# One core, attention followed by two expert layers: loads laid out as single stretches, the first expert of the second layer picked from an incomplete sum, and routing steps placed later

## The chip, the cores and the metric

The kernel runs on one core of one Trainium2 chip. The metric is the device time of one execution in microseconds (us), and lower is better. The median of three runs of the kernel before is 150.59 us (150.51 to 150.84).

## The reference

The computation has three parts, one after the other, on 1536 tokens of 512 numbers (float32).

1. A decaying linear attention over blocks of 64 positions gives `x`.
2. A soft mixture of 8 experts with 4 slots each: `slot_input = softmax_over_tokens(x @ phi).T @ x`, then per expert `relu(slot_input[e] @ w1[e]) @ w2[e]`, then `x = softmax_over_slots(x @ phi) @ slot_out`. The weights `moe_w1` and `moe_w2` are 32 MB.
3. A hard mixture of 8 experts: each token goes to the expert with the largest gate, at most `capacity` = 384 tokens per expert, others stay zero:

```
expert_idx = argmax(x @ w_gate)
h = relu(disp @ w1); y = h @ w2
out[i] = gate_w[i] * y[expert_idx[i], pos[i]]   # kept tokens; other rows are 0
```

## The kernel before, in words

**Attention** (lines 182 to 273). Twelve units (6 stretches of 128 positions, 2 batches), written out by hand in one order for all engines (`manual_schedule`, line 335). For unit n the TensorE (PE) order is: scores, transposes of the next unit's k, transposes of the last unit's result, the product with the running state, the state's own update (`kv`, line 239), the product with v. VectorE (DVE) makes the decay tables `T` (line 168) from `lamf`, which lies in the small load `pgs`; each half of a unit's scores is multiplied with `T` (line 217), and `kd` (line 198) also needs `T`, so that in the first unit the first `kv` waits for `pgs`, both halves of `T` and `kd`.

**Loads.** All loads go through SyncE's (SP's) one queue, in order. A buffer of 1 MB (a "granule", `[128, 2, 1024]`) holds two units' worth of k, q or v, or a quarter of an expert's two matrices. Lines 94 to 103 load the first pair in pieces: k, q, `pgs` and v of batch 0 (256 KB each, 512 columns of each row of 2048), then k, q, v of batch 1, then the second column half (512 KB each). Lines 110 to 131 load the weights, 1 MB each; the last expert's `w2` is cut by columns into two pieces of 512 KB and four of 256 KB (line 122), which in memory are strips of the rows of one granule. The `Z`, `F` and `slt` steps (384 to 421) and the 16 `layer1`/`layer2` blocks (433 to 463) stream the 32 MB through PE.

**The last expert's layer 2** is done in three column parts: `layer2(7, 0)` makes columns 0 to 255 (bank `S[0]`), `layer2(7, 1)` columns 256 to 383 (`S[1]`, which holds all of columns 256 to 511 of the experts before), `layer2(7, 2)` columns 384 to 511 (`S[2]`). `sum_groups` (588) turns the scaled sums `Sp` into `SR`: the slots' outputs (three copies) and, in the last column, token 0's own output. `gate_slots` (592) multiplies the last column with `w_gate` into `l0` (token 0's eight gates) and the slots with `w_gate` into `gp`.

**Choice of the first expert** (620 to 627). The arg max of `l0` goes through a register on SP (`value_load`), and `load_expert` issues this expert's 4 MB in ten pieces (571 to 575): `w1` and `w2` in turn, four of 256 KB, then six of 512 KB. The write of zeros to the rows past `capacity` (`rest`, 565, 2304 KB) is issued on the same queue before them. If the choice were not the expert of all tokens, the loop at line 920 would run a pass for each other expert that has tokens.

**Routing on VectorE**: `gp` is copied to `G`, six matmuls `lps` (633) give all tokens' gates, then `rank_experts` (649), `first_gates` (657, with one Exp on ScalarE) and `split_gate` (667) follow ahead of `first_expert`. PE runs matmuls on zeros ("fillers", `keep_warm`, line 79) in the meantime.

**First expert** (714 to 837). Per quarter j: `project` (PE `pq`), ScalarE's rounded copy and VectorE's remainder `pr` (745), `add_parts` (PE `ph`, 750, needs `pr`), `pp`, `hidden` (PE `hq`, ScalarE `ht`, VectorE `ht` low part 774), the splitting of `w2` (ScalarE 754, VectorE 757), and the `output` matmuls (783). PE works these off in the written order, so `ph` of a quarter stands in front of the outputs that follow it. After quarter j one routing step is called (816): `count_tokens`, `rank_active`, `list_active`.

Fillers ahead of the first expert are counted in `WR`: `WR[3]` is 24.

Of the kernel before, what the change touches and what calls it, by code (L numbers as in the profile page):

```python
# [21 lines left out]
P = 128  # L22
# [10 lines left out]
NU = SEQ // P  # L33
NR = NU // 2
W0 = (20, 3, 5)
WR = (3, 2, 4, 24, 20)
WARM = (4, 2, 2, 3)
both = (0, 1)
BIG = 16384.0
SC = 32768.0  # L40
# [10 lines left out]
def tile_kernel(ctx: ExitStack, tc: tile.TileContext, q, k, v, pg, w1, w2,  # L51
# [34 lines left out]
    wgs = pgs[:, NK * NS:NK * (NS + NE)].rearrange("p (k s) -> p k s", k=NK)  # L86

    stage = []  # L90
    for u in range(0, NU, 2):
        pair = {nm: granule(f"{nm}st{u}") for nm in "kqv"}
        stage += [{nm: pair[nm][:, c].rearrange("p (b n) -> p b n", b=B) for nm in "kqv"} for c in range(2)]

        if u == 0:
            parts = [(0, slice(512 * b, 512 * b + 512)) for b in range(B)] + [(1, slice(0, 1024))]
        else:
            parts = [(slice(0, 2), slice(0, 1024))]
        for c, cols in parts:
            for nm, src in (("k", k), ("q", q), ("v", v)):  # L100
                nc.sync.dma_start(out=pair[nm][:, c, cols], in_=src[u // 2][:, c, cols])
                if nm == "q" and u == 0 and c == 0 and cols.start == 0:
                    nc.sync.dma_start(out=pgs, in_=pg)

    wtiles = {}
# [6 lines left out]
    def load_weights(n):  # L112
        for _ in range(n):
            if wnext[0] == len(wlist):
                return
            j0 = wnext[0]
            which, e, j = wlist[j0]
            wnext[0] += 1
            g = granule(f"w{which}_{e}_{j}", pool=pools[j0 % len(pools)])
            src = (w1 if which == 1 else w2)[e, j]  # L120

            n = (1 if (which, e) != (2, NE - 1) else (2, 4)[j])
            w = 2048 // n
            gf, sf = g.rearrange("p c n -> p (c n)"), src.rearrange("p c n -> p (c n)")
            for c in range(n):
                nc.sync.dma_start(out=gf[:, w * c:w * c + w], in_=sf[:, w * c:w * c + w])
            for c in range(2):
                t = g[:, c]
                if which == 2 and e < NE - 1:
                    t = t.rearrange("p (c n) -> p c n", c=2)  # L130
                wtiles[(which, e, 2 * j + c)] = t
# [318 lines left out]
    def layer2(e, j=None, fcs=range(NF)):  # L450
        for fc in fcs:
            g, a = fc // 2, fc % 2
            cg = fc % 4
            for z in range(2) if j is None else (j,):
                if j is None:
                    wt = wtiles[(2, e, g)][:, a, 256 * z:256 * z + 256]
                elif j == 0:
                    wt = wtiles[(2, e, fc // 4)][:, 256 * cg:256 * cg + 256]
                else:
                    wt = wtiles[(2, e, j + 1)][:, P * fc:P * fc + P]  # L460
                dst = S[z][32 * cg:32 * cg + 32, 0:P if j else 256]
                nc.tensor.matmul(dst, hTs[e][:, a, NS * g:NS * g + NS], wt,  # L462
                                 start=fc < 4 and (e == 0 or j == 2), stop=e == NE - 1 and fc >= 4)

    nst = cap // P
    layer1(0)
# [93 lines left out]
            for t in range(4):  # L560
                nc.vector.tensor_copy(stc[NS * t:NS * t + NS, 3 * NS:], cT[0:NS, 0, 0:1])


    rest = out[cap:, :].rearrange("(p r) d -> p r d", p=P)
    nc.sync.dma_start(out=rest, in_=bcast(zrow, 1, (NTOK - cap) // P))

    def load_expert(ev):
        m1, m2 = [granule("m1") for _ in range(2)], [granule("m2") for _ in range(2)]
        t1, t2 = [[g[:, c] for g in m for c in range(2)] for m in (m1, m2)]

        parts = [(t, 0, 512 * h, 512) for h in both for t in (t1, t2)]
        parts += [(t, j, 0, 1024) for j in range(1, 4) for t in (t1, t2)]
        for t, j, c, w in parts:
            src = mw1 if t is t1 else mw2
            nc.sync.dma_start(out=t[j][:, c:c + w], in_=src[ds(ev, 1), j, :, c:c + w].rearrange("e p n -> p (e n)"))  # L575
# [14 lines left out]
    def gate_slots(dst, lhs, kcs):  # L590
        for kc in kcs:
            nc.tensor.matmul(dst, lhs(kc), wgs[:, kc, :], start=kc == 0, stop=kc == NK - 1)

    e = NE - 1
    layer2(e, 0)
    nc.scalar.activation(Sp[:, 0:2].rearrange("p k n -> p (k n)"), S[0], AF.Copy, scale=rsum)
    layer2(e, 1)
    nc.vector.tensor_scalar(out=Sp[:, 2:4].rearrange("p k n -> p (k n)"), in0=S[1], scalar1=rsum,
                            scalar2=None, op0=ALU.mult)
    layer2(e, 2, range(4))  # L600
# [4 lines left out]
    nc.vector.scalar_tensor_tensor(out=Sp[:, 3], in0=S[2], scalar=rsum, in1=Sp[:, 3],  # L605
                                   op0=ALU.mult, op1=ALU.add)
    nc.scalar.copy(SR[:, 0:3], srp[0])

    keep_warm(WR[0], "qk", 2)
    sum_groups(3)  # L610
    nc.vector.tensor_copy(SR[:, 3:4], srp[1])
    y0 = lambda kc: SR[:, kc, 3 * NS:]
    slot = lambda kc: SR[:, kc, 0:NS]
    gate_slots(l0, y0, range(3))
    keep_warm(WR[1], "qk", 2)
    gate_slots(gp, slot, range(2))
    gate_slots(l0, y0, (3,))
    gate_slots(gp, slot, (2, 3))
    keep_warm(WR[2], "sc1")
    m0 = bpool.tile([1, NE], F32, name="m0")  # L620
    nc.vector.max(out=m0, in_=l0)
    e0i = bpool.tile([1, NE], U32, name="e0i")
    nc.vector.max_index(out=e0i, in_max=m0, in_values=l0)
# [19 lines left out]
    mx = bpool.tile([P, NT], F32, name="mx")  # L643
    vr = bpool.tile([P, NT, NE], F32, name="vr")
    vm = bpool.tile([P, NT], F32, name="vm")
    nc.vector.tensor_reduce(out=mx, in_=lgs, axis=AX.X, op=ALU.max)

    def rank_experts():
        nc.vector.tensor_tensor(out=vr, in0=lgs, in1=bcast(mx, 2, NE), op=ALU.is_equal)
        nc.vector.tensor_tensor(out=vr, in0=vr, in1=bcast(rank8, 1, NT), op=ALU.mult)  # L650
        nc.vector.tensor_reduce(out=vm, in_=vr, axis=AX.X, op=ALU.max)
# [62 lines left out]
    def first_expert(t1, t2):  # L714
# [81 lines left out]
        hidden(1)  # L796
        split_w2(1)
        hidden_low()
        for z in (1, 2):
            for s in range(nst):  # L800
                output(0, s, (z,))
        for j in range(3):
            project(j + 1)
            steps = [(2 * j, s) for s in range(nst) if j] + [(2 * j + 1, s) for s in range(nst)]
            for n, (fc, s) in enumerate(steps):
                output(fc, s)
                left = len(steps) - 1 - n
                if left == (3 if j else 2):
                    add_parts(j + 1)
                    split_w2(2 * j + 2)  # L810
                if left == (1 if j else 0):
                    for f in (2 * j + 2, 2 * j + 3):
                        hidden(f)
                        hidden_low()
                    split_w2(2 * j + 3)
            (count_tokens, rank_active, list_active)[j]()
        nv = nc.values_load(nact[0:1, 0:1], min_val=0, max_val=NE)
        for s in range(nst):
            output(NF - 2, s)
# [16 lines left out]
        keep_warm(WR[4], "lg")  # L836
        return nv

    rank_experts()
    first_gates()  # L840
    split_gate()
    nv = first_expert(*ew)
    ordered.close()

# [82 lines left out]
def arrays(inputs):  # L927
# [3 lines left out]
    named = [("q", heads["q"].reshape(B, NK, 2, NU, P, D).transpose(3, 2, 5, 0, 1, 4))]  # L931
    named += [(n, heads[n].transpose(2, 3, 0, 1, 4)) for n in "kv"]

    pairs = lambda a: np.reshape(a, a.shape[:-3] + (a.shape[-3] // 2, 2, P, 1024)).swapaxes(-3, -2)
    named = [(n, pairs(a.reshape(NU, P, B * DM))) for n, a in named]

    pg = [np.reshape(inputs[n], (NK, P, -1)).transpose(1, 0, 2).reshape(P, -1)
          for n in ("moe_phi", "moe2_w_gate")]
# [6 lines left out]
    w2 = np.concatenate([w2[:NE - 1], np.stack([a.reshape(P, 1024) for a in last])[None]])
    named += [("moe_w2", pairs(w2))]
    m1 = np.reshape(inputs["moe2_w1"], (NE, NK, P, 4, 2, P)).transpose(0, 3, 2, 4, 1, 5)
    m2 = np.reshape(inputs["moe2_w2"], (NE, 4, 2, P, DM)).transpose(0, 1, 3, 2, 4)
    named += [("moe2_w1", m1.reshape(NE, 4, P, 1024)), ("moe2_w2", m2.reshape(NE, 4, P, 1024))]
# [19 lines left out]
```

## Time and profile before

| what | value |
|---|---|
| median of 3 runs | 150.59 us (150.51 to 150.84) |
| the profiled execution's own time | 151.13 us |
| its span (first to last instruction) | 148.9 us |
| PE busy | 137.3 us (92%) |
| VectorE busy | 80.1 us (54%) |
| ScalarE busy | 43.1 us (29%) |
| mean granted PE clock | 0.985 of 2.4 GHz |
| moved by DMA | 50.70 MB, mean 341 GB/s |

The span starts with the first instruction and ends with the last; some 2.2 us of the execution's time lie around it. Engines: PE is the matmuls, PEld the weight loads of PE, which run ahead of them and show best when PE really waited; DVE is VectorE, ACT ScalarE, SPq the queue of SyncE that issues transfers. An arrow in brackets names what ended an engine's wait and how long the wait was. A transfer's rate is read from the table by stretches, where "DMA share" is the mean busy share of 16 DMA engines.

### The profile page before, as it was taken

How to read it: one execution, taken by the hardware profiler on the slowest of the kernel's cores; microseconds unless marked ns; L12 is line 12 of the kernel's file. 1: busy time of each engine (PE TensorE's matmuls, PEld its weight loads, DVE VectorE, ACT ScalarE, POOL GpSimd, SP SyncE). 2: the span in 40 equal slices, each digit the busy share in tenths (PEclk: the TensorE clock that was granted, in tenths of full speed). 3: DMA queues.
4: the chain of work that ended last, by engine and by line, in shares of the span. 5: the costliest groups of instructions: out<-in, count | busy, mean ns of one | idle time of the engine just before them, and what ended most of it. 6: DMA issues, size and time to landing. Idle time of an engine off the chain costs nothing.

```text
span 148.9 us, 4091 instructions
## 1 busy us (share of the span) xinstructions
PE 137.3 (92%) x1688; PEld 103.0 (69%) x1688; DVE 80.1 (54%) x193; ACT 43.1 (29%) x101; POOL 18.7 (13%) x39
## 2 busy tenths in 40 slices
PE   7829999999999999998899999999989898999990
PEld 5619888888688886976464665555647785778880
DVE  2496778966977896733437312111223645866810
ACT  3111424414233343234213001111112253463340
POOL 5004313440431200010003400000000000000000
PEclk9995999999999999999999999999999999999998
DMA  3899999999999999999999999999998889500041
GB/s 115 236 375 430 425 420 425 416 420 412 423 418 420 423 414 423 418 420 416 407 401 431 414 423 416 423 416 390 358 405 332 243 262 418 209 4 0 2 163 55
DMA packets 10692, 50.70 MB, mean 341 GB/s; under 512 B 1072, under 2 KB 1456, under 8 KB 6064
## 3 DMA queue, kind: packets, MB, share of 16 engines
q1 hardware_dynamic: 10528, 50.29, 85.2%
q8 instruction: 14, 0.23, 0.6%
q10 hardware_dynamic: 144, 0.13, 0.3%
q14 instruction: 6, 0.05, 0.1%
HBM read 47.27 MB, written 3.15 MB: 339 GB/s over the span
## 4 chain that ended last, share of the span: by engine, by line
PE 59%; DMA 26%; DVE 8%; SPq 2%; issue 2%; ACT 1%; DVEq 0%
DMA w<-in_moe_w_dram 19%; PE yp L783 9%; PE sp L209 8%; PE op L256 7%; PE op L228 7%; DMA m<-in_moe_w_dram 4%; PE kv L239 4%; PE hp L437 4%; PE kps L187 4%; PE xp L270 3%; PE wp L79 3%; DMA pgs<-in_pg_dram 3%; PE slp L320 2%; DVE T L168 2%; SPq L575 1%
## 5 line engine op out<-in xcount | busy, mean ns | idle before, releaser
L783 PE MATMUL yp<-wt,ht 128*128 128x512 f32 (+1 forms) x96 | 18.9, 342 | 0.0
L217 DVE TENSOR_TENSOR AT<-sp,T 128x512 f32<-128x512 f32 x24 | 15.5, 685 | 3.6 <-PE sp L209 3.1
L783 PEld LDWEIGHTS yp<-wt,ht 128*128 128x128 f32 x96 | 15.0, 189 | 3.3 <-DVE ht L774 0.5
L248 POOL TENSOR_TENSOR dec<-st,R 64x256 f32<-64x256 f32 x16 | 12.6, 785 | 34.2 <-DVE st L245 20.6
L462 PE MATMUL S<-w,hT 128*32 128x256 f32 (+1 forms) x272 | 16.4, 372 | 0.4 <-DMA w<-in_moe_w_dram 0.4
L437 PE MATMUL hp<-w,Z 128*32 128x256 f32 x256 | 15.5, 381 | 0.0
L209 PEld LDWEIGHTS sp<-qst,kT 64*128 64x128 f32 x192 | 12.3, 196 | 4.1 <-issue 1.8
L209 PE MATMUL sp<-qst,kT 64*128 64x128 f32 x192 | 14.6, 293 | 0.3 <-ACT kT L189 0.3
L256 PE MATMUL op<-AT,vst 128*64 128x128 f32 x192 | 13.7, 287 | 0.5 <-ACT xT L265 0.5
L79 PE MATMUL wp<-wsrc 128*128 128x256 bf16 x87 | 13.0, 300 | 1.1 <-DVE wsrc L74 1.1
L265 ACT COPY xT<-op 128x512 f32<-128x512 f32 (+1 forms) x13 | 7.2, 553 | 21.9 <-PE op L256 21.9
L462 PEld LDWEIGHTS S<-w,hT 128*32 128x32 f32 x272 | 8.7, 109 | 6.0 <-DMA w<-in_moe_w_dram 1.8
L189 ACT COPY kT<-kps 128x512 f32<-128x512 f32 x12 | 7.0, 586 | 18.6 <-PE kps L187 18.6
L256 PEld LDWEIGHTS op<-AT,vst 128*64 128x64 f32 x192 | 11.0, 145 | 1.0 <-ACT xT L265 0.7
L437 PEld LDWEIGHTS hp<-w,Z 128*32 128x32 f32 x256 | 8.3, 110 | 4.6 <-issue 0.2
L448 DVE COPY hT<-tp 128x256 f32<-128x256 f32 x8 | 3.3, 415 | 14.7 <-PE tp L446 14.7
L79 PEld LDWEIGHTS <-wsrc 128*128 128x128 bf16 x87 | 8.8, 108 | 3.2 <-DVE wsrc L74 1.1
L228 PE MATMUL op<-qd,st 128*128 128x128 f32 x80 | 10.9, 280 | 0.0
L245 DVE TENSOR_TENSOR st<-dec,kv 64x256 f32<-64x256 f32 x16 | 6.7, 419 | 7.1 <-PE kv L239 6.9
L228 PEld LDWEIGHTS op<-qd,st 128*128 128x128 f32 x80 | 9.7, 191 | 0.8 <-issue 0.8
L202 DVE TENSOR_TENSOR qd<-qst,R 128x512 f32<-128x512 f32 x10 | 9.8, 982 | 0.7 <-PE op L228 0.6
L187 PE MATMUL kps<-ident,kst 128*128 128x128 f32 x48 | 7.8, 285 | 1.7 <-DMA kst<-in_k_dram 1.7
(173 smaller groups left out, 160.5 us busy)
## 6 DMA issues: line engine op xcount, KB each, us to landing
w<-in_moe_w_dram SPq DMA_DIRECT2D x30, 1024.0 KB, 18.3
m<-in_moe_w_dram SPq DMA_DIRECT2D x6, 512.0 KB, 8.2
out_dram<-zrow SPq DMA_DIRECT2D x1, 2304.0 KB, 13.4
kst<-in_k_dram SPq DMA_DIRECT2D x2, 1024.0 KB, 12.4
qst<-in_q_dram SPq DMA_DIRECT2D x2, 1024.0 KB, 14.0
vst<-in_v_dram SPq DMA_DIRECT2D x2, 1024.0 KB, 15.0
w<-in_moe_w_dram SPq DMA_DIRECT2D x2, 512.0 KB, 18.1
w<-in_moe_w_dram SPq DMA_DIRECT2D x4, 256.0 KB, 13.0
```

The costliest lines, as they stand in the source:

```text
L79: nc.tensor.matmul(wp[:, 0:256], wsrc[:, 0:P], wsrc, start=True, stop=True)
L187: nc.tensor.transpose(ps[:, a, :], w["k"][:, P * a:P * a + P], ident)
L202: nc.vector.tensor_tensor(out=w["qd"], in0=w["q"], in1=R, op=ALU.mult)
L209: nc.tensor.matmul(sp[h2][:, a, :], w["kT"][hrows[h2], a, :], w["q"][hrows[h2], a, :], start=True, stop=True)
L217: nc.vector.tensor_tensor(out=t, in0=sp[h2], in1=tab, op=ALU.mult)
L228: nc.tensor.matmul(w["op"][:, a, :], st[b][:, a, :], w["qd"][:, a, :], start=a == 0, stop=False, skip_group_check=True)
L248: nc.gpsimd.tensor_tensor(out=dec[b][r], in0=st[b][r, :, r], in1=bcast(R[r, :, P - 1], 2, D), op=ALU.mult)
L256: nc.tensor.matmul(w["op"][hrows[h2], a, :], w["v"][:, D * (2 * a + h2):D * (2 * a + h2 + 1)], w["AT"][h2][:, a, :], start=u == 0 and a == ...
L265: nc.scalar.copy(xts[n][:, pairs], work[n]["op"][:, pairs])
L437: nc.tensor.matmul(hp[32 * g:32 * g + 32, :], Zf[:, kc, NS * e:NS * e + NS], wtiles[(1, e, kc)][:, 256 * g:256 * g + 256], start=kc == 0, ...
L462: nc.tensor.matmul(dst, hTs[e][:, a, NS * g:NS * g + NS], wt, start=fc < 4 and (e == 0 or j == 2), stop=e == NE - 1 and fc >= 4)
L783: nc.tensor.matmul(dst, ht[:, a, P * s:P * s + P], rhs, start=(fc, z) == (0, 0), stop=(fc, z) == (NF - 1, 2))
```

## The change

Every DRAM array is laid out on the host so that each load reads one unbroken stretch; the tiles in on-chip memory stay as they are. The first k, q and v are now loaded by 512 KB (both batches at once) and `pgs` stands behind k and q of that size. The expert's ten pieces become eight: `w1` and `w2` in turn, of 256, 256, 512 and 1024 KB.

The first expert is now chosen from `yg`, token 0's output without the last expert's share in columns 256 to 511: `guess_first` uses `Sp[:, 0:2]` and `Sg`, a scaled copy of `S[1]` before `layer2(7, 1)`. The gates `l0` and the arg max follow inside `layer2(7, 1)`. The write of zeros is issued behind `load_expert`. `rank_experts` moves behind the first expert's second `hidden_low`, `first_gates` in front of `rank_active` (after quarter 1) and `split_gate` behind `list_active`. `WR[3]` goes from 24 fillers to 4.

```diff
-WR = (3, 2, 4, 24, 20)
+WR = (3, 2, 4, 4, 20)
+WG = (3, 3, 2, 4)
...
+    def load(out, src, at):
+        w = out.shape[-1]
+        nc.sync.dma_start(out=out, in_=src[at:at + P * w].rearrange("(p n) -> p n", p=P))
...
-        for c, cols in parts:
+        n = 1 if u == 0 else 2
+        for c in range(0, 2, n):
             for nm, src in (("k", k), ("q", q), ("v", v)):
-                nc.sync.dma_start(out=pair[nm][:, c, cols], in_=src[u // 2][:, c, cols])
-                if nm == "q" and u == 0 and c == 0 and cols.start == 0:
+                load(pair[nm][:, c:c + n].rearrange("p c n -> p (c n)"), src[u // 2], P * 1024 * c)
+                if nm == "q" and u + c == 0:
                     nc.sync.dma_start(out=pgs, in_=pg)
...
-    rest = out[cap:, :].rearrange("(p r) d -> p r d", p=P)
-    nc.sync.dma_start(out=rest, in_=bcast(zrow, 1, (NTOK - cap) // P))
...
+        for z, at, w in ((0, 0, 512), (0, 512, 512), (0, 1024, 1024), (1, 0, 2048)):
+            for m, src in ((m1, mw1), (m2, mw2)):
...
+    def guess_first():
+        g0 = bank([P, NK], "qk", 2, "g0")
+        for kc in range(NK):
+            nc.tensor.matmul(g0[:, kc:kc + 1], Sp[:, kc, :] if kc < 2 else Sg[:, kc - 2, :],
+                             stc[:, 3 * NS:], start=True, stop=True)
+        nc.vector.tensor_copy(yg, g0)
...
-    layer2(e, 1)
+    nc.vector.tensor_scalar(out=Sg.rearrange("p k n -> p (k n)"), in0=S[1], scalar1=rsum, scalar2=None,
+                            op0=ALU.mult)
+    keep_warm(WG[0], "sc1")
+    guess_first()
+    layer2(e, 1, range(4))
+    gate_slots(l0, lambda kc: yg[:, kc:kc + 1], range(NK))
+    layer2(e, 1, range(4, NF))
+    m0 = bpool.tile([1, NE], F32, name="m0")
+    nc.vector.max(out=m0, in_=l0)
+    e0i = bpool.tile([1, NE], U32, name="e0i")
+    nc.vector.max_index(out=e0i, in_max=m0, in_values=l0)
...
-    gate_slots(l0, y0, range(3))
-    keep_warm(WR[1], "qk", 2)
-    gate_slots(gp, slot, range(2))
-    gate_slots(l0, y0, (3,))
-    gate_slots(gp, slot, (2, 3))
-    keep_warm(WR[2], "sc1")
+    keep_warm(WG[2], "qk", 2)
+    gate_slots(gp, slot, range(NK))
+    keep_warm(WG[3], "sc1")
...
     ew = load_expert(e0)
+
+    rest = out[cap:, :].rearrange("(p r) d -> p r d", p=P)
+    nc.sync.dma_start(out=rest, in_=bcast(zrow, 1, (NTOK - cap) // P))
...
         hidden_low()
+        rank_experts()
...
-            (count_tokens, rank_active, list_active)[j]()
+            for step in ((count_tokens,), (first_gates, rank_active), (list_active, split_gate))[j]:
+                step()
...
-    rank_experts()
-    first_gates()
-    split_gate()
     nv = first_expert(*ew)
```

## Rows read from the trace of the kernel before

**Rows 1.** Busy time by stretches: each engine's us, granted clock, DMA share, GB/s.
```profile
10.00:13.00 3.00, 2.10 (x31) 2.10 (x32) 2.94 (x9) 0.30 (x1) 0.48 (x1) 0.72 1.03 425
81.00:100.00 19.00, 19.00 (x308) 11.23 (x301) 4.16 (x16) 2.45 (x7) 2.32 (x10) 1.00 1.01 419
```

**Rows 2.** Timeline, PE's weight loads: the last expert's layer 2 (start, us).
```profile
107.79 0.16 PEld L462 LDWEIGHTS S<-w,hT 128*32 128x32 f32 x8 [0.33 <-DMA w<-in_moe_w_dram]
109.72 0.16 PEld L462 LDWEIGHTS S<-w,hT 128*32 128x32 f32 x8 [0.49 <-DMA w<-in_moe_w_dram]
```

**Rows 3.** Timeline, the first attention unit.
```profile
5.65 0.34 DVE L146 COPY lamp<-pgs 64x4 f32<-64x4 f32 x2 [3.58 <-DMA pgs<-in_pg_dram]
6.19 1.16 PE L209 MATMUL sp<-qst,kT 64*128 64x128 f32 x16 [0.35 <-ACT kT L189]
7.48 0.69 DVE L217 TENSOR_TENSOR AT<-sp,T 128x512 f32<-128x512 f32 x1
10.90 0.82 PE L239 MATMUL kv<-vst,kd 128*64 128x64 f32 x16 [1.22 <-DVE kd L198]
```

**Rows 4.** Busy time by stretches, for the rate of the loads (last column).
```profile
4.00:6.00 2.00, 1.84 (x15) 1.33 (x12) 0.33 (x2) 0.45 (x1) 0.00 (x0) 1.00 0.87 242
119.00:120.00 1.00, 0.81 (x6) 0.73 (x7) 0.68 (x2) 0.75 (x2) 0.00 (x0) 1.00 0.98 150
122.00:123.00 1.00, 1.00 (x7) 0.79 (x5) 0.25 (x1) 0.72 (x2) 0.00 (x0) 1.00 1.04 422
```

**Rows 5.** Timeline, from the last sums to the first expert, and eight earlier matmuls (L411).
```profile
73.67 1.07 PE L411 MATMUL slt<-F,acc 128*128 128x32 f32 x8
...
108.50 0.47 ACT L596 ACTIVATE Sp<-S,rsum 128x256 f32<-128x256 f32 x1 [2.58 <-PE S L462]
...
110.08 0.52 PEld L588 LDWEIGHTS srp<-stc,Sp 128*128 128x128 f32 x4 [0.20 <-issue]
...
110.69 0.16 PEld L462 LDWEIGHTS S<-w,hT 128*32 128x32 f32 x8
...
112.00 0.30 PE L592 MATMUL l<-pgs,SR 128*1 128x8 f32 x6
...
113.21 0.15 DVE L623 FIND_INDEX8 e0i<-m,l 1x8 uint32<-1x8 f32 x1
...
113.76 0.74 PEld L633 LDWEIGHTS lps<-G,cT 128*128 128x128 f32 x6 [0.47 <-ACT G L625]
...
114.42 7.03 SPq L575 DMA_DIRECT2D m<-in_moe_w_dram  x10
...
114.85 2.52 PEld L79 LDWEIGHTS <-wsrc 128*128 128x128 bf16 x24
...
117.38 0.93 PEld L736 LDWEIGHTS ph<-m,SR 128*96 128x96 f32 x8
```

**Rows 6.** Timeline, the routing steps on VectorE, and the first expert's second quarter.
```profile
115.03 0.24 DVE L646 TENSOR_REDUCE mx<-lgs 128x12 f32<-128x96 f32 x1
...
116.07 0.17 DVE L658 TENSOR_TENSOR ge<-lgs,mx 128x24 f32<-128x24 f32 x1
...
117.30 0.52 DVE L670 CAST Gs<-G 32x8 fp32r<-32x8 f32 x3
...
123.48 0.56 DVE L774 SCALAR_TENSOR_TENSOR ht<-hq,ht 128x384 fp32r<-128x384 f32 x1
123.77 0.16 PEld L742 LDWEIGHTS pq<-m,SR 128*32 128x32 f32 x8 [0.89 <-DMA m<-in_moe_w_dram]
...
125.36 0.16 PEld L750 LDWEIGHTS ph<-pr,stack 128*96 128x96 f32 x1 [0.24 <-DVE pr L745]
```

**Rows 7.** Timeline, the first expert's last quarter on VectorE and PE.
```profile
134.63 0.16 DVE L696 TENSOR_TENSOR act<-cnt,rk 128x8 f32<-128x8 f32 x1
...
135.51 0.41 DVE L745 TENSOR_TENSOR pr<-pq,pr 128x256 fp32r<-128x256 f32 x1
...
136.03 0.28 PEld L750 LDWEIGHTS ph<-pr,stack 128*96 128x96 f32 x2
```

More of the change, by code (lines that the diff above doesn't have):

```diff
@@ L93, in tile_kernel @@
         stage += [{nm: pair[nm][:, c].rearrange("p (b n) -> p b n", b=B) for nm in "kqv"} for c in range(2)]
[L95 to L98, printed above, removed]
-        for c, cols in parts:
+        n = 1 if u == 0 else 2
+        for c in range(0, 2, n):
             for nm, src in (("k", k), ("q", q), ("v", v)):
-                nc.sync.dma_start(out=pair[nm][:, c, cols], in_=src[u // 2][:, c, cols])
-                if nm == "q" and u == 0 and c == 0 and cols.start == 0:
+                load(pair[nm][:, c:c + n].rearrange("p c n -> p (c n)"), src[u // 2], P * 1024 * c)
+                if nm == "q" and u + c == 0:
                     nc.sync.dma_start(out=pgs, in_=pg)
@@ L123, in load_weights @@
             w = 2048 // n
-            gf, sf = g.rearrange("p c n -> p (c n)"), src.rearrange("p c n -> p (c n)")
+            gf = g.rearrange("p c n -> p (c n)")
             for c in range(n):
-                nc.sync.dma_start(out=gf[:, w * c:w * c + w], in_=sf[:, w * c:w * c + w])
+                load(gf[:, w * c:w * c + w], src, P * w * c)
             for c in range(2):
@@ L462, in layer2 @@
                 nc.tensor.matmul(dst, hTs[e][:, a, NS * g:NS * g + NS], wt,
-                                 start=fc < 4 and (e == 0 or j == 2), stop=e == NE - 1 and fc >= 4)
+                                 start=fc < 4 and (e == 0 or j == 2),
+                                 stop=fc >= 4 and (e == NE - 1 or (e == NE - 2 and z == 1)),
+                                 skip_group_check=j == 1)
     nst = cap // P
@@ L569, in load_expert @@
         t1, t2 = [[g[:, c] for g in m for c in range(2)] for m in (m1, m2)]
[L571 to L575, printed above, removed]
+        for z, at, w in ((0, 0, 512), (0, 512, 512), (0, 1024, 1024), (1, 0, 2048)):
+            for m, src in ((m1, mw1), (m2, mw2)):
+                o = P * (2048 * z + at)
+                nc.sync.dma_start(out=m[z].rearrange("p c n -> p (c n)")[:, at:at + w],
+                                  in_=src[ds(ev, 1), o:o + P * w].rearrange("e (p n) -> p (e n)", p=P))
         return ([g.rearrange("p (h k f) -> p h k f", h=2, k=NK) for g in t1],
@@ L592, in gate_slots @@
             nc.tensor.matmul(dst, lhs(kc), wgs[:, kc, :], start=kc == 0, stop=kc == NK - 1)
+    Sg = bpool.tile([P, 2, P], F32, name="Sg")
+    yg = bpool.tile([P, NK], F32, name="yg")
+    def guess_first():
[4 more added lines that the diff above has]
+        nc.vector.tensor_copy(yg, g0)
     e = NE - 1
@@ L607, in tile_kernel @@
     nc.scalar.copy(SR[:, 0:3], srp[0])
-    keep_warm(WR[0], "qk", 2)
+    keep_warm(WG[1], "qk", 2)
     sum_groups(3)
     nc.vector.tensor_copy(SR[:, 3:4], srp[1])
-    y0 = lambda kc: SR[:, kc, 3 * NS:]
     slot = lambda kc: SR[:, kc, 0:NS]
-    gate_slots(l0, y0, range(3))
-    keep_warm(WR[1], "qk", 2)
-    gate_slots(gp, slot, range(2))
-    gate_slots(l0, y0, (3,))
-    gate_slots(gp, slot, (2, 3))
-    keep_warm(WR[2], "sc1")
[L620 to L623, printed above, removed]
+    keep_warm(WG[2], "qk", 2)
+    gate_slots(gp, slot, range(NK))
+    keep_warm(WG[3], "sc1")
     for t in range(4):
@@ L645, in tile_kernel @@
     vm = bpool.tile([P, NT], F32, name="vm")
-    nc.vector.tensor_reduce(out=mx, in_=lgs, axis=AX.X, op=ALU.max)
     def rank_experts():
+        nc.vector.tensor_reduce(out=mx, in_=lgs, axis=AX.X, op=ALU.max)
         nc.vector.tensor_tensor(out=vr, in0=lgs, in1=bcast(mx, 2, NE), op=ALU.is_equal)
@@ L932, in arrays, with pairs, single @@
     named += [(n, heads[n].transpose(2, 3, 0, 1, 4)) for n in "kv"]
-    pairs = lambda a: np.reshape(a, a.shape[:-3] + (a.shape[-3] // 2, 2, P, 1024)).swapaxes(-3, -2)
-    named = [(n, pairs(a.reshape(NU, P, B * DM))) for n, a in named]
+    def pairs(a):
+        a = np.reshape(a, a.shape[:-3] + (a.shape[-3] // 2, 2, P, 1024))
+        return a.swapaxes(-3, -2).reshape(a.shape[:-3] + (-1,))
+    def single(a):
+        return np.concatenate([np.reshape(a[:2], (1, -1)), pairs(a[2:])])
+    named = [(n, single(a.reshape(NU, P, B * DM))) for n, a in named]
     pg = [np.reshape(inputs[n], (NK, P, -1)).transpose(1, 0, 2).reshape(P, -1)
@@ L944, in arrays @@
     last = [last[:, 0:4, 0:256], last[:, 4:8, 0:256], last[:, :, 256:384], last[:, :, 384:512]]
[L945 to L949, printed above, removed]
+    last = [np.reshape(last[0], -1), np.reshape(last[1], -1)] + \
+        [np.reshape(a[:, c:c + 4], -1) for a in last[2:] for c in (0, 4)]
+    w2 = np.concatenate([pairs(w2[:NE - 1]), np.concatenate(last).reshape(1, 2, -1)])
+    named += [("moe_w2", w2)]
+    m1 = np.reshape(inputs["moe2_w1"], (NE, NK, P, 4, 2, P)).transpose(0, 3, 2, 4, 1, 5).reshape(NE, 4, P, 1024)
+    m2 = np.reshape(inputs["moe2_w2"], (NE, 4, 2, P, DM)).transpose(0, 1, 3, 2, 4).reshape(NE, 4, P, 1024)
+    for n, a in (("moe2_w1", m1), ("moe2_w2", m2)):
+        parts = [a[:, 0, :, 0:512], a[:, 0, :, 512:], a[:, 1], pairs(a[:, 2:])]
+        named.append((n, np.concatenate([np.reshape(x, (NE, -1)) for x in parts], 1)))
     return [(n, np.ascontiguousarray(a)) for n, a in named]
```

## The prediction

> **What bounds the kernel now.** I read the table by stretches first, then the timeline of each place that the change touches. In the weight stage PE is busy without a gap and the DMA engines are full as well (19.00 us of 19, DMA share 1.01 [rows 1]): two chains run side by side. Where they meet, the last expert's layer 2, PE comes only 0.33 us ahead of the second half of its first matrix strip, whose work starts at 107.79, and falls further behind the loads from there to 109.72 [rows 2]. So a faster stream of loads is worth 0.33 us there and no more; after that PE's own chain, which began with the first `kv` at 10.90 [rows 3], sets the time. That chain hangs on `pgs`: VectorE starts on it at 5.65 and works through the tables and both products without a rest until `kd` frees PE [rows 3]. Behind 107.79 come the choice of the expert, the loads' first arrival at 117.38 [rows 5], one more wait for a load of 0.89 us at 123.77 [rows 6], and then a first expert in which PE is always busy, but near VectorE's time for `pr` [rows 7].
>
> **The change part by part**, as shifts against the profiled execution. Its own time is 151.13 us, a span of 148.9 and 2.2 around it; that is 0.54 over the median of 150.59, so I apply the sum of shifts to the median. A measurement can tell about 0.2%, 0.3 us, from no change.
>
> *Loads as stretches, weight stage.* Full granules already run at 419 GB/s [rows 1]. In strips of 2 KB per row the rate is 242 GB/s at the start and 150 in the tail; unbroken 512 KB pieces run at 422 [rows 4]. The strips seem to be what is slow, since both kinds have the DMA engines 0.87 to 1.04 busy. So the stream comes out earlier, PE's wait goes, and PE is late next: **-0.33**.
>
> *Loads as stretches, the start.* This part can cost. Before, `pgs` stood behind k and q of 256 KB: 610 KB with itself. Now it stands behind 512 KB each: 1135 KB. At 242 GB/s that is 4.69 us against 2.52, so `pgs` and all of PE's chain come 2.17 later; if the new loads run at 422 it takes 2.69, 0.17 later. A gain is nearly excluded: the first product at 7.48 also needs the scores, which end at 7.35 (6.19 + 1.16), and these wait for k's copy [rows 3]. Bounds -0.1 and +2.2. I take **+0.1**: 4 KB rows without gaps are the form of the 422 row, and part of the landing time at the start is a fixed delay.
> The Trainium skill (Perfetto Trace Analysis, Contiguity and DMAs) says that contiguity matters to a transfer only within a partition's line in on-chip memory. By that nothing in the DRAM layout helps, the rate at the start stays 242 and this term is about +2; the trace speaks against it, with 150 and 422 GB/s for pieces that differ in it, though the two also differ in length of row.
>
> *PE's clock at the start.* The granted clock averages 0.72 in 10 to 13 [rows 1], a mix of its two levels, after VectorE kept PE waiting. PE now does the second unit's transposes earlier and waits in one piece, so the drop stays. I cost a change at nothing; with no drop at all it would be -0.8 (0.28 of 3 us), with a drop as long again +0.8, and these are the bounds.
>
> *Choice and routing.* Call the start of `layer2(7, 0)`'s second half X. Before, PE got from X to the first expert in 117.38 - 107.79 = 9.59 us. After, on PE: the copy `Sp` ends 108.50 + 0.47 - 107.79 = 1.18 after X, with three fillers and `Sg` beside it; `guess_first` is eight matmul passes with 128x128 weights, like the eight of L411, 1.0; four and four passes of `layer2(7, 1)` take 0.36 each (109.72 to 110.08) and hide the copy `yg`; the gates `l0`, eight passes, 0.35 (six took 0.30); half of `layer2(7, 2)` 0.36; the first sums 0.61 (110.08 to 110.69) [rows 2, 5]. That is X + 4.3. From there to `lps` it took 113.76 - 110.69 = 3.07; without the passes of `l0` 2.8. From `lps` to the first expert 3.62, of which 24 fillers were 2.52; with four it is 1.5 [rows 5]. Sum X + 8.6: **-1.0**.
> Is the load there by then? The arg max ends 0.4 behind `l0`, at X + 3.4; from its end to the first issue is 114.42 - 113.36 = 1.06, and from there to use at most 117.38 - 114.42 = 2.96 [rows 5]: X + 7.4. So the loads are no longer what ends last, by over a microsecond, and the earlier choice pays only this 1.0. The 2304 KB of zeros lie behind the expert's 4 MB; nobody waits for them, and at 422 GB/s both are through in 16 us, before the outputs are written. On SP's queue only the output writes stand behind them.
>
> *First quarter of the expert.* The wait of 0.89 at 123.77 [rows 6] goes. But `rank_experts` now stands on VectorE behind `ht`, which ends at 124.04, 6.66 after the first expert's start. Its four steps take 116.07 - 115.03 = 1.04, then `pr` 0.41 [rows 6, 7]: `ph` can run 8.15 after the start. Before, it ran at 125.36 - 117.38 = 7.98 [rows 6], load wait included. PE reaches `ph` earlier and stands still. Net **+0.2**; if hidden, -0.9.
>
> *Third quarter.* `first_gates` goes in front of `rank_active`. VectorE has just finished the `w2` split at 134.63 and has no gap up to `pr`, which ends at 135.92, and PE asks for `ph` at 136.03 [rows 7]. The steps took 117.30 - 116.07 = 1.23, ScalarE's Exp in their middle, for which VectorE waits [rows 6]. With about 0.2 of slack for the second half of `ph`: **+1.0**; bounds 0 and 1.3. `split_gate` is three casts and a subtraction, 0.7, behind the last `pr`, beside PE's output matmuls: nothing.
>
> Sum: -0.33 + 0.1 - 1.0 + 0.2 + 1.0 = -0.03. **Forecast 150.5**: what the earlier load wins is given back on VectorE.
>
> **The rivals.** *A, VectorE's steps don't show*: should PE arrive at `ph` later than I reckon, the +1.0 goes and the time is 149.5; if +0.2 becomes -0.9 too, 148.4. Against it: VectorE runs without a gap into both `pr`. For it: PE's order has other waits that I don't see.
> *B, slower: the tables come late.* Mechanism: `pgs` behind twice the bytes. It decides from a rate at the start under about 360 GB/s, where 1135 KB take 3.15 us and the term is +0.6. At 300 GB/s it is +1.26 and the time 151.7; at 242 it is 152.6. This is also the case in which unbroken loads do not do what they are laid out for; the skill's sentence above would be its reason. For it: the start row is the slowest long stretch. Against it: the 422 row.
> *C, the choice is wrong.* The sum lacks the last expert's share in half of the columns. With the reference's arithmetic on its own inputs the left-out share moves the gates by 0.17 of the largest where the lead is 0.32 (seed 0), and the arg max was the same for seven of eight seeds. If wrong, a second expert is run: at least the 31.5 us from 117.38 to the span's end, 182 us.
>
> **How the numbers follow.** Forecast 0.56, with its own range 149.9 to 151.1 from terms of some 0.3 us each; it holds faster 0.18, same 0.28, slower 0.10. A 0.20, all faster. B 0.22 and C 0.02, all slower. So faster 0.38, same 0.28, slower 0.34. The range 149.4 to 151.9 takes in A's first value and B's middle one; it leaves out A's second, B's end and C.
>
> **What would show it.** The first unit: VectorE's work on `pgs` starts 5.6 to 5.9, and the rate from 2 to 8 us near 400. PE no longer waits for loads in layer 2. The first issue of the expert's load comes about 4.5 us after X, PE's fillers end after the load has landed, and the first expert starts near 116.1. The wait at `pq` is gone, and `ph` waits for VectorE's `pr` by about 1 us in the first and third quarter. It is wrong if `pgs` lands after 6.5, if these waits are not there, if the first expert still starts on a load, or if a second expert is loaded.

## The result, and the profile after

The changed kernel takes 149.43 us (median of 20 executions) where the kernel before took 151.45 (20): ratio 0.987 [0.984, 0.9901]. It is faster by 1.3%; the forecast was no change. The profiled executions are closer to each other: span 147.8 against 148.9, own time 149.71 against 151.13. Ratios, and the table that follows, leave out executions more than 1.5% above the quickest of the same kernel; the two medians take in all 20.

Sorted by mean granted clock, the medians of the spans are (the changed kernel in the executions just named, the kernel before in those that were timed beside the experiments, on three chips):

| | mean granted clock 0.995 and over | mean granted clock 0.984 to 0.989 |
|---|---|---|
| before | 148.95 (22) | 149.4 (25) |
| after | 146.65 (8) | 147.85 (10) |

In the profiles a mean of 0.984 to 0.989 goes with one stretch at 1.2 GHz at the start; of the other executions only the mean is on record. Two things are to be seen. The change gains 1.55 us at the lower clock and 2.3 us at the higher: the changed kernel keeps more of what a full clock gives. (How much the kernel before gains by it is less sure: 0.3 to 1.05 us on the three chips, 0.45 in all.) And the profile of before, 148.9, is one of the quick executions of its column.

The page of the changed kernel: busy tenths in 40 slices, granted clock, DMA share, rate.

```profile
span 147.8 us, 4058 instructions
PE   7918999999999999998799999999999897998992
PEclk9995999999999999999999999999999999999999
DMA  5999999999999999998999999999932999970033
GB/s 171 333 417 427 417 426 426 417 419 412 419 421 417 417 419 424 415 375 310 421 361 424 428 426 410 419 415 418 397 114 68 280 350 388 404 297 0 2 110 107
```

The table by stretches (us, PE, PEld, DVE, ACT, POOL, granted clock, DMA share, GB/s), to be read against [rows 1, 4]:

```profile
2.00:4.00 2.00, 2.00 (x11) 1.41 (x10) 0.06 (x1) 0.20 (x2) 0.72 (x2) 1.00 0.95 346
4.00:6.00 2.00, 1.74 (x15) 1.29 (x12) 0.00 (x0) 0.55 (x1) 0.00 (x0) 1.00 0.94 275
6.00:8.00 2.00, 1.75 (x20) 1.39 (x20) 1.49 (x6) 0.16 (x2) 0.00 (x0) 1.00 1.03 403
...
10.00:13.00 3.00, 1.26 (x20) 1.26 (x22) 2.88 (x8) 0.00 (x0) 0.00 (x0) 0.68 1.03 434
60.00:80.00 20.00, 18.56 (x243) 13.07 (x243) 9.12 (x23) 6.13 (x18) 1.35 (x2) 1.00 0.97 379
```

and three of the same windows in the kernel before:

```profile
2.00:4.00 2.00, 2.00 (x11) 1.42 (x10) 0.06 (x1) 0.20 (x1) 0.72 (x2) 1.00 0.80 232
6.00:8.00 2.00, 1.16 (x16) 0.97 (x16) 1.89 (x5) 0.13 (x1) 0.00 (x0) 1.00 0.96 265
60.00:80.00 20.00, 18.55 (x241) 12.99 (x243) 9.12 (x23) 6.13 (x18) 1.35 (x2) 1.00 1.01 413
```

The new loads do come faster at the start: 346 GB/s in 2 to 4 us against 232, 275 in 4 to 6 against 242, and 403 in 6 to 8 against 265. Over 60 to 80 us the rate is lower than before (379 against 413): the loads are ahead by then. One that is issued at the same time in both, at 80.68 before and 80.76 after, when a buffer comes free, lands after 14.4 us before and 13.9 after.

The start of the changed kernel, against [rows 3]:

```profile
6.49 0.34 DVE L149 COPY lamp<-pgs 64x4 f32<-64x4 f32 x2 [4.42 <-DMA pgs<-in_pg_dram]
...
11.74 0.48 PE L242 MATMUL kv<-vst,kd 128*64 128x64 f32 x4 [3.90 <-DVE kd L201]
```

`pgs` and `kv` come 0.84 us later. Yet PE's first layer 1 of the experts starts at 75.28, where it was 75.20. The half-clock stretch covers the same time but less work, so by the scores of PE's third unit 0.51 of the 0.84 is left (18.10 against 17.59). VectorE then waits 0.42 us longer in the kernel before, ahead of the state's update at 31.41 (1.11 us there, 0.69 after), and at 35 us the lag is 0.1.

The last expert's layer 2 and the choice, from PE's weight loads and the timeline of all engines, against [rows 2, 5]:

```profile
105.61 2.35 PEld L465 LDWEIGHTS S<-w,hT 128*32 128x32 f32 x48 [0.17 <-issue]
108.38 0.22 PEld L80 LDWEIGHTS <-wsrc 128*128 128x128 bf16 x3 [0.41 <-issue]
109.02 0.52 PEld L603 LDWEIGHTS g<-stc,Sp 128*128 128x128 f32 x4 [0.42 <-ACT Sp L609]
...
110.99 0.15 DVE L620 FIND_INDEX8 e0i<-m,l 1x8 uint32<-1x8 f32 x1
...
112.61 4.67 SPq L575 DMA_DIRECT2D m<-in_moe_w_dram  x8
...
114.36 0.74 PEld L650 LDWEIGHTS lps<-G,cT 128*128 128x128 f32 x6 [0.48 <-ACT G L639]
...
115.45 0.33 PEld L80 LDWEIGHTS <-wsrc 128*128 128x128 bf16 x4
...
115.80 0.93 PEld L753 LDWEIGHTS ph<-m,SR 128*96 128x96 f32 x8
```

No weight load waits for `w`. The step that finds the index starts at 110.99 instead of 113.21, and the load is issued at 112.61 instead of 114.42. Its first piece lands 2.5 us later, at 115.1, and the first expert starts at 115.80, 1.58 us earlier than before, behind four fillers. The first and third quarter, against [rows 6, 7]:

```profile
123.81 0.16 PEld L767 LDWEIGHTS ph<-pr,stack 128*96 128x96 f32 x1 [1.09 <-DVE pr L762]
...
133.10 0.17 DVE L675 TENSOR_TENSOR ge<-lgs,mx 128x24 f32<-128x24 f32 x1
133.31 0.22 ACT L676 ACTIVATE ge<-ge 128x24 f32<-128x24 f32 x1 [0.89 <-DVE ge L675]
...
134.19 0.22 DVE L680 SCALAR_TENSOR_TENSOR gw<-vm,sel,gw 128x3 f32<-128x3 f32 x1
134.33 0.16 DVE L713 TENSOR_TENSOR act<-cnt,rk 128x8 f32<-128x8 f32 x1
...
135.21 0.42 DVE L762 TENSOR_TENSOR pr<-pq,pr 128x256 fp32r<-128x256 f32 x1
135.68 0.16 PEld L767 LDWEIGHTS ph<-pr,stack 128*96 128x96 f32 x1 [0.71 <-DVE pr L762]
```

PE stands still for `pr`, 1.09 and 0.71 us, where it stood 0.24 [rows 6] and nothing [rows 7] before: the wait for a load in the second quarter is gone, and these have come.

### The profile page after: what moved, and what is told of

Its sections match the earlier page's. It is cut to its first block, busy times and chain, and to the rows that moved or that the text cites. A ratio compares the mean times of both kernels' runs of the same rounds, so it can differ in the third digit from the quotient of the medians.

```text
span 147.8 us, 4058 instructions
## 1 busy us (share of the span) xinstructions
PE 135.7 (92%) x1679; PEld 102.1 (69%) x1679; DVE 80.6 (55%) x195; ACT 42.9 (29%) x101; POOL 18.7 (13%) x39
## 4 chain that ended last, share of the span: by engine, by line
PE 80%; DVE 10%; DMA 3%; ACT 3%; issue 1%; SPq 1%; DVEq 0%
PE S L465 10%; PE hp L440 10%; PE sp L212 8%; PE op L259 8%; PE op L231 7%; PE yp L800 7%; PE kv L242 5%; PE kps L190 4%; PE xp L273 4%; DMA pgs<-in_pg_dram 3%; PE wp L80 3%; PE slp L323 2%; PE lT L291 2%; PE tp L449 2%; DVE T L171 2%; DVE ht L791 2%
## 5 line engine op out<-in xcount | busy, mean ns | idle before, releaser
L212 PEld LDWEIGHTS sp<-qst,kT 64*128 64x128 f32 x192 | 11.6, 187 | 4.1 <-issue 1.8
L212 PE MATMUL sp<-qst,kT 64*128 64x128 f32 x192 | 13.9, 285 | 0.3 <-ACT kT L192 0.3
L80 PE MATMUL wp<-wsrc 128*128 128x256 bf16 x70 | 11.2, 305 | 1.1 <-DVE wsrc L75 1.1
L451 DVE COPY hT<-tp 128x256 f32<-128x256 f32 x8 | 3.3, 415 | 14.7 <-PE tp L449 14.7
L242 PE MATMUL kv<-vst,kd 128*64 128x64 f32 x160 | 7.3, 237 | 3.9 <-DVE kd L201 3.9
L242 PEld LDWEIGHTS kv<-vst,kd 128*64 128x64 f32 x160 | 5.9, 146 | 5.3 <-DVE kd L201 4.1
```

Source lines behind the costliest of these rows:

```text
L212: nc.tensor.matmul(sp[h2][:, a, :], w["kT"][hrows[h2], a, :], w["q"][hrows[h2], a, :], start=True, stop=True)
L242: nc.tensor.matmul(kv[hrows[h2], a, :], w["kd"][:, 2 * a + h2, :], w["v"][:, D * (2 * a + h2):D * (2 * a + h2 + 1)], start=True, stop=True)
```

## The experiments

Ratios are to the kernel before, on the same chip.

**1 and 2. The loads alone, and all but the loads.** First the kernel before with the new load code and layout:

```diff
-                nc.sync.dma_start(out=gf[:, w * c:w * c + w], in_=sf[:, w * c:w * c + w])
+                load(gf[:, w * c:w * c + w], src, P * w * c)
```

(and the same for k, q, v and the chosen expert); then the changed kernel with the old loads and layout.

> The kernel before with every load as one stretch (the expert's load in eight pieces) and nothing else of the change. Theory 1 (the gain is made in the tail, by the earlier choice and the load of the expert coming before PE needs it): the start loses about 0.8 us on pgs and gets most of it back before layer 2, the wait of 0.33 us in layer 2 goes, the first expert still starts about 117 behind the zeros: 0 to 0.7 us faster than the kernel before. Theory 2 (much of the timed gain is made at the start, where the unbroken loads change what PE does before its clock is set): 1 us or more faster, with a higher granted clock in the runs.

> The changed kernel with all loads and the arrays' layout as before, so the choice, the order of the zeros and VectorE's steps alone. Theory 1: the first expert starts about 116 if the strips of the expert's load land in time, 1 to 1.5 us faster than the kernel before after the stall in the third quarter is paid; about 0 to 0.7 slower than the full change. Theory 2: within 0.5 us of the kernel before, since the start is as before.

Measured: the loads alone 0.9925 [0.9867, 0.9982], all but the loads 0.9956 [0.9914, 0.9998]. The product, 0.988, is the change, so the two parts add up; the intervals are too wide to tell which is the larger. The first gains some 1.1 us, where its first theory had 0 to 0.7, and the second some 0.7, where its first theory had 1 to 1.5. In the first the stream's rate over 60 to 80 us is 369 GB/s and the first expert still starts late, at 118.83 in its profile, since PE still waits 2.57 us in sum for the last pieces of `w` (0.30, 0.62, 1.19, 0.46): the new loads alone do not take these waits away. In the second the first expert starts at 115.75, as in the full change, behind one wait of 1.02 us for `w` at 107.74.

**3. The routing steps behind `pr` instead of in front of it.** In the changed kernel:

```diff
-        rank_experts()
...
+            for step in ((rank_experts,), (count_tokens,), (rank_active, first_gates))[j]:
+                step()
...
-            for step in ((count_tokens,), (first_gates, rank_active), (list_active, split_gate))[j]:
-                step()
+        list_active()
+        split_gate()
```

> The changed kernel with each routing step moved behind VectorE's next pr (rank_experts behind the second quarter's, count_tokens behind the third's, rank_active and then first_gates behind the last one's; list_active and split_gate at the end). Theory 1: PE's waits for pr (1.1, 0.4 and 0.7 us on the weight loads) shrink to under 0.3 each and the kernel is 1 to 2 us faster than the changed one, some 3 us faster than the kernel before. Rival: the steps delay pp instead and PE waits as long at hq: within 0.4 us of the changed kernel.

Measured: 147.92 us, ratio 0.9724 [0.9649, 0.9799], span 145.8. Its timeline:

```profile
115.97 0.93 PEld L753 LDWEIGHTS ph<-m,SR 128*96 128x96 f32 x8
...
123.14 0.16 PEld L767 LDWEIGHTS ph<-pr,stack 128*96 128x96 f32 x1 [0.24 <-DVE pr L762]
...
133.48 0.28 PEld L767 LDWEIGHTS ph<-pr,stack 128*96 128x96 f32 x2
```

The first expert starts 0.17 us later than in the change, the second `ph` comes 0.67 us earlier (123.14 against 123.81), the one of the third quarter runs without a wait, and PE's last fillers start 2.0 us earlier (140.59 against 142.59). So the waits for `pr` were on the path and cost 2 us. The forecast had 1.2 for its two terms, but these are what the change adds; the 2 us hold also waits that the kernel before has already (0.24 in the second quarter, 0.36 in the third). This version beats both kernels.

**4 and 5. `pgs` ahead of all loads**, in the changed kernel and in version 3:

```diff
+    nc.sync.dma_start(out=pgs, in_=pg)
...
-                if nm == "q" and u + c == 0:
-                    nc.sync.dma_start(out=pgs, in_=pg)
```

> The changed kernel with the small load pgs issued first instead of third. If the late pgs (VectorE starts on it at 6.49 instead of 5.65) costs the whole kernel what it costs the first kv, the kernel is 0.8 us faster than the changed one. If the clock and the wait near 31 us take it back, as the two traces suggest, it is within 0.4 us of the changed one.

> The routing steps behind pr (147.9 us in its run, against 152.0 for the kernel before) together with pgs issued first. If the start does not matter, as pgs first alone showed, it is within 0.4 us of the routing steps alone, 2.5 to 3 per cent faster than the kernel before. If pgs counts once the stalls behind it are gone, it is 0.5 us faster than those.

Measured: 0.9881 [0.9822, 0.994] and 0.9753 [0.9689, 0.9817], as without the edit. The first `kv` came at 11.06 instead of 11.74, and layer 1 at 74.89 instead of 75.28: 0.4 us in the profile, too little for the timing to show. The late tables cost nothing that can be measured.

**6 and 7. The zeros.** `rest` is the write of the zeros. In the changed kernel `rest` is written ahead of `load_expert`, as before; in the kernel before it is moved behind `load_expert`. For the first:

```diff
+    rest = out[cap:, :].rearrange("(p r) d -> p r d", p=P)
+    nc.sync.dma_start(out=rest, in_=bcast(zrow, 1, (NTOK - cap) // P))
     def load_expert(ev):
...
     ew = load_expert(e0)
-    rest = out[cap:, :].rearrange("(p r) d -> p r d", p=P)
-    nc.sync.dma_start(out=rest, in_=bcast(zrow, 1, (NTOK - cap) // P))
```

> The changed kernel with the 2304 KB of zeros issued where they were, before the expert's load. Theory (the zeros share the DMA engines with the last weights and stand before the expert's load): PE waits again for the last pieces of w2, up to 1 us, and the first expert starts on its load, at about 117.5 instead of 115.8: 1 to 2 us slower than the changed kernel. Rival (the strips, not the zeros, made the last weights late, and the earlier choice alone brings the load in time): within 0.4 us of the changed kernel.

> The kernel before with the write of zeros issued behind the expert's load and nothing else. Theory: the waits for the last pieces of w2 shrink and the wait of 0.89 us at the second quarter's pq goes, but the first expert still starts behind 24 fillers and a late choice, near 117: 0.5 to 1.2 us faster than the kernel before. Rival (the zeros only fill a queue that is idle while the choice is made): within 0.4 us.

Measured: zeros first in the changed kernel 1.0059 [1.0009, 1.0109], 1.9% over the change (1.0059 / 0.987); zeros last in the kernel before 1.0008 [0.9959, 1.0057]. So the zeros' place is worth nothing alone, and all of the gain once the fillers are few: ten of 13 executions with the zeros ahead were granted a mean clock of 0.976 or less. (The ratio rests on five of the 13; the medians of all are 153.08 and 152.2 us.) The one profile, of the slowest of them (157.07 us), has the load issued at 114.00 instead of 112.61 and PE waiting 1.01 us for `w` at 109.15. It shows the clock at 0.50 from 112 to 128 us, so it fell ahead of the first expert; whether the others lost it there or in front of a late load isn't seen.

In the second, the waits for `w` stayed, though with the zeros out of their way the stream had brought all but 0.2 of 43.3 MB by 108 us. PE's weight loads, and the table by stretches:

```profile
107.69 0.16 PEld L462 LDWEIGHTS S<-w,hT 128*32 128x32 f32 x8 [1.05 <-DMA w<-in_moe_w_dram]
108.32 0.16 PEld L462 LDWEIGHTS S<-w,hT 128*32 128x32 f32 x8 [0.48 <-DMA w<-in_moe_w_dram]
108.99 0.16 PEld L462 LDWEIGHTS S<-w,hT 128*32 128x32 f32 x8 [0.51 <-DMA w<-in_moe_w_dram]
109.63 0.16 PEld L462 LDWEIGHTS S<-w,hT 128*32 128x32 f32 x8 [0.49 <-DMA w<-in_moe_w_dram]
...
108.00:109.00 1.00, 0.76 (x18) 0.17 (x11) 0.00 (x0) 0.47 (x1) 0.00 (x0) 1.00 0.35 123
109.00:110.00 1.00, 0.78 (x17) 0.31 (x17) 0.48 (x1) 0.00 (x0) 0.00 (x0) 1.00 0.14 53
```

The last pieces, of 256 KB, come 0.63 to 0.67 us apart.

**8. The choice from the full sum, at its old place**, in the changed kernel, which leaves the four fillers:

```diff
-    guess_first()
-    layer2(e, 1, range(4))
-    gate_slots(l0, lambda kc: yg[:, kc:kc + 1], range(NK))
-    layer2(e, 1, range(4, NF))
+    layer2(e, 1)
...
+    gate_slots(l0, y0, range(3))
```

> The changed kernel with the choice of the expert made from the full sum, at its old place; loads, zeros, fillers and routing steps as changed. Theory (the earlier choice is needed to have the load there when PE comes): the choice is known some 1.5 to 2 us later, PE has nothing to do until the load lands, and the kernel is 0.8 to 1.6 us slower than the changed one. Rival (without guess_first's matmuls in its way PE and the load come at the same time as before): within 0.4 us of the changed kernel.

**9. The same with 24 fillers, and 10. the changed kernel with 24 fillers:**

```diff
-WR = (3, 2, 4, 4, 20)
+WR = (3, 2, 4, 24, 20)
```

> Edit: as the run with the choice taken from the full sum at its old place, with 24 fillers in front of the first expert in place of 4. Theory 1 (that run lost 3% because PE stood still in front of the first expert and its clock fell there): the 20 fillers take about 2 us, PE's wait for the load drops from 2.25 us to under 0.7, the clock stays at its full level, and the time comes back to within 0.3 us of the kernel before or somewhat under it: ratio 0.990 to 1.000. Theory 2 (the late load is the loss, whatever PE does meanwhile): the first expert starts no earlier, and the ratio stays at 1.010 to 1.020.

> Edit: the changed kernel with 24 fillers in front of the first expert in place of 4, nothing else. Theory 1 (the prediction's term: the earlier choice pays through the 20 fillers that it makes needless): the first expert starts 1.0 us later, near 116.8, and the time is 1.0 us over the change's, ratio to the kernel before about 0.993. Theory 2 (the fillers are hidden by something that ends as late, for instance the table of kept tokens or the loads): the first expert starts at 115.8 to 116.1 and the ratio stays at 0.987. Theory 3 (with fewer fillers the clock falls in some executions): the ratio is under 0.987.

Measured, as ratios:

| | 4 fillers | 24 fillers |
|---|---|---|
| choice without the upper columns | 0.987 [0.984, 0.9901] (the change) | 1.0021 [0.998, 1.0062] |
| choice from the full sum | 1.0164 [1.0102, 1.0227] | 1.0017 [0.9972, 1.0062] |

With 24 fillers it does not matter which choice is made. The early choice pays by the fillers that it makes needless; without it, taking them out makes the kernel slower by 1.5% (1.0164 / 1.0017). Version 8 is 3.0% slower than the change (1.0164 / 0.987), some 4.4 us, where I had expected 0.8 to 1.6 or nothing. Why shows in the tables by stretches, first of 8, then of 9:

```profile
112.00:116.00 4.00, 2.21 (x16) 1.54 (x15) 0.82 (x6) 0.61 (x4) 0.00 (x0) 0.97 0.31 94
116.00:118.00 2.00, 1.63 (x8) 1.63 (x8) 0.00 (x0) 0.00 (x0) 0.00 (x0) 0.50 0.88 224
118.00:122.00 4.00, 3.33 (x13) 2.84 (x13) 1.74 (x4) 1.53 (x4) 0.00 (x0) 0.50 1.04 412
```

```profile
112.00:116.00 4.00, 3.81 (x33) 3.23 (x32) 0.77 (x5) 0.53 (x4) 0.00 (x0) 1.00 0.29 87
116.00:118.00 2.00, 1.40 (x13) 1.10 (x11) 0.28 (x1) 0.57 (x2) 0.00 (x0) 1.00 0.96 314
118.00:122.00 4.00, 3.94 (x26) 3.26 (x30) 1.90 (x5) 2.00 (x5) 0.00 (x0) 1.00 1.05 366
```

In 8 PE waits for the load, is busy for 2.21 us of 4, and then works at 1.2 GHz (0.50) through the start of the first expert. In 9 the fillers keep it busy and the clock stays at 2.4. The two first experts start at the same time, and what differs is the speed behind it. PE's weight loads in 8 and in 9:

```profile
113.79 0.33 PEld L80 LDWEIGHTS <-wsrc 128*128 128x128 bf16 x4
116.37 1.68 PEld L742 LDWEIGHTS ph<-m,SR 128*96 128x96 f32 x8 [2.25 <-DMA m<-in_moe_w_dram]
```

```profile
113.71 2.52 PEld L80 LDWEIGHTS <-wsrc 128*128 128x128 bf16 x24
116.28 0.90 PEld L742 LDWEIGHTS ph<-m,SR 128*96 128x96 f32 x8
```

In 10 the 24 fillers take 2.52 us in front of a load that is there, and the first expert starts at 118.28, of which 0.3 us were lost ahead of layer 2. I had expected the twenty fillers to cost 1.0 us: that was the net of the whole term, in which the twenty fillers alone are 2.1.

**11 and 12. Both kernels, unchanged, profiled a second time.**

> Edit: none; the kernel before, profiled a second time on another chip. Theory 1 (the time from the last write's issue to the end of the program hangs on the layout of the loads): 5.0 to 5.1 us, as in the first profile (143.82 to 148.9), and not 4.5 as in the changed kernel (143.30 to 147.8). Theory 2 (it is by chance): it may fall on either value. The waits for w in the last expert's layer 2 add up to 0.5 to 2.5 us and differ from those of the first profile.

> Edit: none; the changed kernel, profiled a second time. Theory 1 (as for the kernel before, profiled again): 4.4 to 4.6 us from the last write's issue to the end of the program. Theory 2 (by chance): it may fall near 5.05. No wait for w in the last expert's layer 2, or one under 0.3 us, since the stretches give the stream its reserve.

Measured: spans 150.1 (granted clock 0.989) and 146.5 (0.999). The weight loads of the last expert's layer 2, in the kernel before and in the changed one:

```profile
106.80 0.61 PEld L462 LDWEIGHTS S<-w,hT 128*32 128x32 f32 x16 [0.57 <-DMA w<-in_moe_w_dram]
108.00 0.19 PEld L462 LDWEIGHTS S<-w,hT 128*32 128x32 f32 x8 [0.59 <-issue]
109.76 0.16 PEld L462 LDWEIGHTS S<-w,hT 128*32 128x32 f32 x8 [1.57 <-DMA w<-in_moe_w_dram]
```

```profile
106.55 0.16 PEld L465 LDWEIGHTS S<-w,hT 128*32 128x32 f32 x8 [0.34 <-DMA w<-in_moe_w_dram]
107.12 0.22 PEld L80 LDWEIGHTS <-wsrc 128*128 128x128 bf16 x3 [0.41 <-issue]
107.78 0.52 PEld L603 LDWEIGHTS g<-stc,Sp 128*128 128x128 f32 x4 [0.44 <-ACT Sp L609]
```

The kernel before now waits 3.65 us in sum for `w` (0.57, 1.57, 0.49, 0.52, 0.50), where its first profile had 1.78 and I had expected 2.5 at most, and its first expert starts at 119.39 instead of 117.38. The changed kernel comes to its layer 2 1.3 us earlier than in its first profile, at full clock, and waits 0.34. Version 9 has the same loads and comes to its layer 2 at the same time (104.29 in both); there PE waits 1.91 us for `w` (0.50, 0.45, 0.47, 0.49). So the work of the early choice, put between the parts of layer 2, fills 1.6 us of these waits, whatever the layout. It takes longer than they did: `lps` starts at 113.12 in the changed kernel and at 112.62 in 9. The gain is the fillers behind it, as the table above has it.

## Why the prediction was wrong

The mechanisms forecast for the tail took place; the sum was wrong. That 149.43 us lies inside the range of 149.4 to 151.9, and on rival A's first value, is luck: the shift of -0.03 was put on a median of 150.59 from three executions, where the later 20 have 151.45, and rival A's mechanism did not take place. In the kernel before these weight loads stand ahead of X:

```profile
105.54 1.92 PEld L462 LDWEIGHTS S<-w,hT 128*32 128x32 f32 x40 [0.17 <-issue]
```

Step by step against the profiled pair:

- *The wait in layer 2, with the start* (forecast -0.33 and +0.1, together -0.23). In the kernel before the forty weight loads ahead of X took 1.92 us; counted so from 105.61, X is now 107.53, for 107.79: -0.26. Right. Rival B's mechanism took place, `pgs` landing 0.84 later, near the 6.5 that I had set as its mark; but it is used up by 75 us, and `pgs` first gives no measurable gain. The rates of the start rose, and the loads alone gain 0.75%. That the layout in DRAM did it is not shown: the first loads are now also twice as large, with rows of 4 KB for 2 KB. Where size and rows are the same in both layouts (the first four pieces of the expert's load), the fourth lands 6.2 to 7.6 us after the first issue in the four profiles with strips and 5.4 to 7.3 in the ten with stretches, which does not tell them apart. The sentence of the Trainium skill (Perfetto Trace Analysis, Contiguity and DMAs) that contiguity matters only within a partition's line is therefore neither borne out nor refuted here.
- *PE's clock at the start* (forecast nothing): one stretch at 1.2 GHz in both profiles, 11.3 to 14.7 us before and 11.1 to 14.5 after. Right.
- *Choice and routing* (forecast X + 8.6, -1.0). It is 115.80 - 107.53 = 8.27, for 9.59: **-1.32**. The load lands before the fillers end, as forecast, though it was issued 5.1 us after X and not 4.5. (In the kernel before 117.38 was the end of the 24 fillers and not the load's arrival, as the prediction has it; the load had landed 2.8 us after its issue, at 117.2.) The first sums came 0.15 sooner than counted (111.68 against X + 4.3), the steps to `lps` 0.12 sooner, and the last stretch 0.06.
- *First quarter* (forecast +0.2): 8.01 us from the first expert's start to the second `ph`, for 7.98: +0.03. *Second*: +0.03, unnamed. *Third* (forecast +1.0): the shift of PE's last fillers is 142.59 - 143.12 = -0.53, so this quarter gave back 0.99. Right, and rival A is refuted: the waits show, and version 3 regains 2 us without them.
- *Behind PE's end*: forecast nothing, measured **-0.57**. From the issue of the last output write to the span's end it took 148.9 - 143.82 = 5.08 us before and 147.8 - 143.30 = 4.50 after. This was in no term.

That is -0.53 - 0.57 = -1.1 on the span, against -0.03: the term for choice and routing was 0.32 too small, and the end, put at nothing, gave 0.57.

The medians differ by another 0.9 us, and there a sentence of the prediction failed: that a faster stream "is worth 0.33 us there and no more". It misread its own rows: it has PE falling "further behind the loads from there to 109.72", but the weight load at 109.72 waits 0.49 us for `w` [rows 2], and the four waits there add up to 1.78. It was also read from one execution, and a quick one. In the second profile of the kernel before the same place costs 3.65 us of waiting. In the old kernel the loads and PE are so level that a PE which is ahead, or a stream that is behind, ends in that wait. In the changed kernel guess, fillers and gates stand where PE would wait for the last pieces; the new loads without them still leave 2.57 us of waiting in version 1 and 1.91 in version 9. The table of spans fits: at the higher clock the kernel before gains 0.45 us and the changed one 1.2. These profiles and medians support it, but how often each wait comes in the kernel before was not counted, so its share of the 0.9 us stays open.

And one term was costed against the wrong other case: taking out 20 fillers was counted as 2.1 us of PE time saved. It is that only if the load is early. Otherwise it costs 1.5%, by the wait for the load and the clock behind it. The prediction asked whether the load would be there, and it was, by 0.7 us where it had counted on 1.2; what it would cost if not, it did not say.

What stays open: why the program's end is shorter with the new loads, and whether their layout, their size or their number is what makes the start faster.

## What to carry over

Where two chains run level, one profile shows only which of them was ahead that time: profile the kernel twice before a wait is taken as the bound of a gain. Fillers in front of a load can go once the load is early, and not sooner. A step that is moved "beside other work" should stand behind the instruction that feeds the bottleneck: on VectorE, behind `pr` and not in front of it, the same steps were 2 us cheaper.

## What I had not expected of the hardware

- The end of the program goes with the load code. From the last write's issue to the span's end it is 5.04 to 5.11 us in the four profiles with strips (the kernel before twice, all but the loads, zeros last) and 4.42 to 4.51 in the ten with stretches, though the writes land 2.1 to 2.3 us after their issue in both kernels. The stretches also come in fewer and partly larger pieces; which of this does it was not tried.
- At the end of a full stream PE's loads stand 0.63 to 0.67 us apart in strips (version 7) and 0.61 to 0.64 apart in 9, with stretches (106.70, 107.31, 107.94, 108.58), each behind a wait for `w`: stretches do not cure this, only other work does. A piece of 256 KB in 0.64 us is 410 GB/s, near the 419 of the full stream [rows 1]: the pieces keep the stream's pace to the end. Yet in version 7 nearly all bytes had come by 108 us, and the DMA share falls to 0.35 and 0.14 in the two us behind it while pieces still land. That a few of the 16 engines are behind the others, and each piece waits for them, would give this; no run here tests it.
- After a wait of 2.25 us in a stretch where PE was busy 2.21 of 4 us, the granted clock was 0.50 for some 6.8 us (115.8 to 122.6, by its shares in the stretches), and the kernel was slower than with 2.5 us of useless matmuls.
